# A key-limit step split from its product, an earlier transpose of v, and two turns less before the own exponentials

## The chip, the core and the metric

The kernel runs on one core of a Trainium2 chip. The metric is the device time of one execution in microseconds (us). The three executions before the change took 990.68, 991.01 and 991.49 us; their median, 991.01 us, is the time before.

## What is computed

Two independent results stand side by side in the output, 512 columns each.

```python
# A: attention with 32 query heads of 16 columns, one shared k and v (2048 rows)
q = (x @ wq) by heads;  k = x @ wk;  v = x @ wv
p = softmax(q @ k.T * 16 ** -0.5)
a = (p @ v, heads side by side) @ wo
# B: gated long convolution of 512 channels over 2048 rows
kv = short_conv(k, shift_k) * v          # 4 taps
b = q * (irfft(rfft(kv) * rfft(ssm_k)) + kv * ssm_D)
out = concatenate([a, b], -1)
```

## The kernel before

**Stacks, tiles and turns.** Attention is cut into 32 stacks (one for four heads and 512 queries). A stack has 16 key tiles of 128 keys, and each makes two score tiles of 128 x 1024. Line 1074 writes a score tile into one of two PSUM buffers "s" (eight matmuls), line 1092 takes its exponential on ScalarE (ACT), and line 1116 multiplies the result with v into a PSUM pair "f" (called `pv`). `attend` walks over the tiles: turn x emits the scores and the exponential of tile x + 2, then the `pv` work that a plan has put into this turn, and then calls `fill.turn`. So a turn is one exponential long, and 32 turns make a stack. Stacks 27 to 30 have only 30 tiles: there the exponentials of the last key tile are computed on VectorE (DVE) by the thread `own`, one stack ahead.

**Fill work.** Everything else (projections, the convolution, the output product) lives in eight generator threads. They yield what they want next: `(n, dve, NEW or CONT, grain)` asks for n units of TensorE work, `(0, dve)` asks for DVE work alone, and `(WAIT, t)` sleeps for 2t turns. `_Fill.turn` (line 1433) goes through the threads in a fixed order (`own` first, then `wo_heads`, `conv_pe`, `conv_short`, `rest_of_q`, `wo_part`, `conv_dve`, `spill`). TensorE work needs room in the turn; work marked NEW also needs that no other thread holds the pair and that a PSUM pair is taken to be free; DVE work needs a positive credit, which grows by 850 a turn and falls by what is charged.

**What sets the order on the chip.** The program order on each engine is the order in which the turns emit. TensorE and DVE take their instructions strictly in that order, so a matmul that needs a DVE result holds up all scores behind it. There are two "f" pairs: one collects the `pv` of the running stack, the other goes from one piece of fill work to the next.

**The places that the change touches.**

- `rest_of_q` in stack 0 (lines 902 to 959): k and v of all keys are finished. `k_chunk(c, bank, h)` (684) multiplies once on TensorE (687), and DVE cuts the result (693), rounds it (700) and writes the key tiles `kst` (702). `v_turn` (704) transposes v on TensorE (709, four transposes) and copies it on DVE (712). `read(less)` (679) sleeps until the planner's estimate of DVE, minus `less`, is due.
- The end of `rest_of_q` (lines 1008 to 1020): the guard of the last x block (306), then `k_max` (670): DVE multiplies and limits four columns (673), TensorE sums them over partitions (674), DVE takes the maximum (677) and finishes with 1018 and 1019. `flag` (1034) follows with three small DVE steps (1041 to 1043), and ten turns later a transpose (1047) and two more (1049, 1050). The prologue calls the same `k_max` at line 848.
- `own` (1155): for stack n in 27 to 30 it waits until slot 32 n - 32 + `OWN_AT` (1168), asks for keys on TensorE twice (1173), and computes on DVE (1174, 1175, 1185, 1188).
- Behind them: at the end of a stack DVE copies the `pv` pair out (1125, 1126), SyncE's queue (SP) stores it (1129); `heads` reads it back and scales it (1248 to 1260, with a load of r at 1255); `wo_part` multiplies with wo (273, by way of `halves`) and DVE scales the result (1312).

Of the kernel before, what the change touches and what calls it, by code (L numbers as in the profile page):

```python
# [14 lines left out]
ALU = mybir.AluOpType  # L15
# [4 lines left out]
P = 128  # L20
# [16 lines left out]
LIM = 10000.0  # L37
# [32 lines left out]
OWN = NKT - 1  # L70
CROWDED = (0, 64), (288, 352)
OWN_IN = (27, 28, 29, 30)
OWN_AT, OWN_PV = 14, 8


def _tables():
# [30 lines left out]
WAIT = -1.0  # L107
NEW, CONT = 0, 1


class _Emit:
# [555 lines left out]
                stop=n == 11 or (c, n) == (3, 7),  # L667
            )

    def k_max(self, b, km):  # L670

        kx = self.ks[:, 4:8]
        self.nc.vector.tensor_scalar(kx, self.msk[:, 291:295], km, LIM, ALU.mult, ALU.min)
        self.nc.tensor.matmul(b, self.msk[:, 0:P], kx, start=True, stop=True)

    def k_row(self, kmr, b):
        self.nc.vector.tensor_reduce(kmr, b, AX.X, ALU.max)
# [87 lines left out]
    def prologue(self):  # L765
# [67 lines left out]
        kh = self.wide()[:, 0, :]  # L833
# [7 lines left out]
        km, kmr = self.ks[:, 0:1], self.ks[:, 1:2]  # L841
# [3 lines left out]
        nc.scalar.activation(qa, cut, AF.Abs)  # L845
        st = self.w.tile([P, 2, 512], F16, tag="st", bufs=2, name=self.nm("st"))
        self.st[0] = st
        self.k_max(kh[:, 0:4], km)
        self.k_first(kb, 0, range(8, 12))
        self.k_row(kmr, kh[:, 0:4])  # L850
        wbn = self.wbn.rearrange("p a (e r) -> p a e r", e=2)[:, :, :, BR]
# [4 lines left out]
        for a in both:  # L856
            b = (self.wide if a else self.pair)()[:, 0, :]
# [44 lines left out]
    def rest_of_q(self):  # L902
# [17 lines left out]
        b = self.pair()  # L920
        sums, rows = b[:, 0, :], b[:, 1, :]
        self.k_chunk(1, rows, 0)
        yield from self.read(700)
        yield 3, 400, CONT, 3
        self.v_turn(slice(0, 96), sums)
        yield from self.read(0)
        yield 2, 1300, CONT, 2
        self.k_chunk(1, rows, 1)
        yield from self.read(700)
# [34 lines left out]
        km, kmr = self.ks[:, 2:3], self.ks[:, 3:4]  # L964
# [7 lines left out]
        while n < 12:  # L972
            g = yield 12 - n, 1400, CONT if n else NEW, 1
            if n == 0:
                b = self.bank()
# [6 lines left out]
        for c in range(4):  # L982
            if c > 1:
                yield from self.after(("x", c))
            for g in (0, 2):
# [5 lines left out]
                if c or g:  # L991
# [4 lines left out]
                    b = yield from self.halves(*work, 1, 1400)  # L996
# [14 lines left out]
            if c < 2:  # L1011
                self.xT[c + 2] = self.w.tile([P, 2, 4, 512], F16, tag="xt", bufs=2, name=f"xT{c + 2}")
        self.qn = 4, 0
        yield 1, 500, NEW, 1
        b = self.bank()[:, 0:4]
        self.k_max(b, km)
        self.k_row(kmr, b)
        v.scalar_tensor_tensor(kmr, self.ks[:, 1:2], -1.015, kmr, ALU.mult, ALU.add)
        v.tensor_scalar(self.gm[:, 3:4], kmr, 1000.0, None, ALU.mult)
# [608 lines left out]
```

## Time and profile before

| what | us |
|---|---|
| three executions, median | 991.01 |
| the profiled execution, its own time | 991.43 |
| its span, first to last instruction | 989.7 |
| ScalarE busy | 951.4 |
| TensorE busy | 941.1 |
| VectorE busy | 747.5 |
| GpSimd busy | 174.0 |

The span leaves out 1.7 us of the profiled execution's own time. A timeline row gives start, length, engine, line, operation, tiles written and read, how many instructions are merged into it, and in square brackets how long the engine had been idle before and whose result ended that. A row of the table by stretches gives the stretch, its length, the busy time of TensorE, its weight loads, VectorE, ScalarE and GpSimd with their instruction counts, then the granted TensorE clock, the share of the DMA engines and GB/s.

### The profile page before, as it was taken

Reading aid. Unit: us, or ns where it says so; the run is one execution under the profiler, and the core shown is the slowest. Engines: PE = TensorE matmul, PEld = TensorE weight load, DVE = VectorE, ACT = ScalarE, POOL = GpSimd, SP = SyncE. Lnnn points to the kernel's source line nnn. Section 1 sums busy time; section 2 is a strip of 40 time slices with the busy share of each in tenths; the row PEclk is TensorE's granted clock in tenths of the full one; section 3 lists DMA queues with packets and bytes.
Section 4 is the critical chain, followed back from the end, with each engine's and each line's share of the span. In section 5 each row is a group of like instructions: output and inputs, shape, how many; then the busy total and the mean of one; then the engine's idle time right before and its main releaser. Section 6 shows DMA issues by size and latency. Waiting matters only on the chain.

```text
span 989.7 us, 51425 instructions
## 1 busy us (share of the span) xinstructions
PE 941.1 (95%) x23565; PEld 463.0 (47%) x23565; DVE 747.5 (76%) x925; ACT 951.4 (96%) x1032; POOL 174.0 (18%) x321
## 2 busy tenths in 40 slices
PE   8999999989999999999899999999979999999996
PEld 5344454435544444444444455544434444444453
DVE  4448686989369989998896578799888936677753
ACT  5799999999999999999999999999979999999995
POOL 6041131411021000100543432000000122211000
PEclk9799999999999999999999999999989999999999
DMA  7153442332133212211543333011221232221101
GB/s 251 57 153 92 121 137 85 107 101 61 29 81 104 81 59 83 79 59 44 155 129 107 96 110 97 22 54 43 61 74 45 75 97 93 81 66 54 40 19 48
DMA packets 69205, 82.93 MB, mean 84 GB/s; under 512 B 20752, under 2 KB 58294, under 8 KB 68982
## 3 DMA queue, kind: packets, MB, share of 16 engines
q1 hardware_dynamic: 47558, 43.48, 14.0%
q0 software_dynamic: 20320, 35.46, 12.1%
q8 instruction: 186, 3.05, 1.3%
q10 hardware_dynamic: 1104, 0.64, 0.2%
q14 instruction: 37, 0.30, 0.1%
HBM read 54.46 MB, written 25.03 MB: 80 GB/s over the span
## 4 chain that ended last, share of the span: by engine, by line
PE 50%; ACT 36%; issue 7%; DVE 6%; DMA 1%; SPq 0%; ACTq 0%; DVEq 0%
ACT p L1092 35%; PE f L1116 23%; PE s L1074 15%; PE f L273 9%; DMA r<-rd 1%; DVE sp L188 1%; ACT xT L630 1%; DVE sp L456 0%; PE f L618 0%; PE f L662 0%; PE f L687 0%; DVE o L1260 0%; PE f L254 0%; DVE ao L1125 0%; ACT pfirst L1092 0%
## 5 line engine op out<-in xcount | busy, mean ns | idle before, releaser
L1092 ACT ACTIVATE p<-s 128x1024 f32<-128x1024 f32 x1008 | 929.9, 1069 | 13.9 <-PE s L1074 12.7
L1116 PE MATMUL f<-p,vx 64*32 64x512 f32 (+1 forms) x8832 | 545.1, 554 | 0.3 <-ACT p L1092 0.3
L1074 PE MATMUL s<-st,kst 49*32 49x512 f16 x8128 | 424.0, 382 | 32.5 <-ACT p L1092 26.8
L1074 PEld LDWEIGHTS <-kst 49*32 49x32 f16 x8192 | 199.0, 89 | 401.9 <-issue 352.9
L1116 PEld LDWEIGHTS f<-p,vx 64*32 64x32 f32 x8832 | 174.0, 106 | 24.7 <-issue 2.7
L313 DVE COPY sp<-f 128x1024 f32<-128x1024 f32 x32 | 39.1, 1222 | 62.1 <-PE f L273 62.1
L188 DVE TENSOR_TENSOR sp<-sp 128x2048 f32<-128x2048 f32 x36 | 82.3, 2287 | 0.9
L318 POOL DMA_DIRECT2D ff<-in_ff x64 | 35.2, 556 | 233.7 <-ACT p L1092 215.3
L273 PE MATMUL f<-wo,o 64*32 64x512 f16 x1440 | 56.2, 375 | 0.3 <-DVE wp L1312 0.2
L273 PE MATMUL f<-xT,wq 64*32 64x512 f16 x1344 | 51.0, 375 | 0.0
L1125 DVE COPY ao<-f 128x512 f32<-128x512 f32 (+1 forms) x33 | 22.2, 674 | 37.5 <-PE f L1116 37.2
L318 POOL DMA_DIRECT2D fi<-in_fi x32 | 17.4, 550 | 182.0 <-ACT p L1092 181.8
L188 DVE TENSOR_TENSOR sp<-sp,sp 128x2048 f32<-128x2048 f32 x19 | 43.4, 2286 | 0.4
L273 PE MATMUL f<-a,ff 64*32 64x256 f32 x1024 | 41.8, 377 | 0.0
L273 PE MATMUL f<-hT,ff 64*32 64x256 f32 x1024 | 40.8, 377 | 0.7 <-DVE hT L367 0.7
L491 POOL DMA_DIRECT2D out<-r x32 | 17.7, 558 | 127.3 <-DVE r L489 117.4
L273 PE MATMUL f<-sp,fi 64*32 64x256 f32 x1024 | 40.0, 376 | 0.0
L489 DVE TENSOR_TENSOR r<-f,q 128x512 f32<-128x512 f32 x16 | 11.0, 689 | 38.0 <-PE f L273 37.9
L428 DVE TENSOR_TENSOR a<-a,t 128x512 f32<-128x512 f32 x48 | 33.1, 690 | 1.5
L419 DVE TENSOR_TENSOR t<-kk,tpb 128x512 f32<-128x512 f32 (+1 forms) x50 | 33.0, 663 | 0.0
L346 POOL DMA_DIRECT2D hin<-in_B_ssm_k x32 | 21.0, 660 | 60.1 <-ACT p L1092 58.6
L1188 DVE SCALAR_TENSOR_TENSOR own<-own,own 128x1024 f32<-128x1024 f32 x24 | 29.4, 1224 | 0.7
(195 smaller groups left out, 790.4 us busy)
## 6 DMA issues: line engine op xcount, KB each, us to landing
ff<-in_ff POOLq DMA_DIRECT2D x64, 128.0 KB, 2.7
od<-ao SPq DMA_DIRECT2D x60, 128.0 KB
qd<-qp SPq DMA_DIRECT2D x48, 128.0 KB
st<-qd SPq DMA_DIRECT2D x62, 98.0 KB
kk<-in_B_k POOLq DMA_DIRECT2D x32, 128.0 KB, 2.6
v<-in_B_v POOLq DMA_DIRECT2D x32, 128.0 KB, 2.6
hin<-in_B_ssm_k POOLq DMA_DIRECT2D x32, 128.0 KB, 5.5
fi<-in_fi POOLq DMA_DIRECT2D x32, 128.0 KB, 2.9
```

The lines of the kernel that those rows point to most:

```text
L188: v.tensor_tensor(out, a, b, op)
L273: y = self.nc.tensor.matmul(out[j : j + 32, cols], w[r, j : j + 32], x[r], start=half == m == 0, stop=half == 1 and m == k - 1,)
L313: self.nc.vector.tensor_copy(out, self.both.rearrange("p i (q n) -> p i q n", q=2))
L318: self.paced(self.nc.gpsimd.dma_start(t[:, i], self.I[n][:, 2 * m2 + i]))
L346: self.paced(nc.gpsimd.dma_start(dst, src))
L419: nc.vector.tensor_tensor(out[:, n], kk[:, x], tap(i, n.stop - n.start), ALU.mult)
L428: nc.vector.tensor_tensor(a, a, t, ALU.add)
L1074: self.nc.tensor.matmul(s[j : j + 32, e, :], self.kst[k // 2][rows, k % 2 * P + j : k % 2 * P + j + 32], self.st[n][rows, a, cols], start= ...
L1092: self.exps[u % 4] = self.nc.scalar.activation(self.pt[u], s, AF.Exp, scale=LN2 * DH**-0.5 / SC / SC)
L1116: nc.tensor.matmul(self.acc[e][32 * j : 32 * j + 32, m], vx[rows, :], y, start=k == 0, stop=stop)
L1125: nc.vector.tensor_copy(a, self.acc[0][:, m])
L1188: v.scalar_tensor_tensor(g, g if i < 4 else y, c[i], y if i else x.bitcast(BF16), ALU.add, ALU.mult)
```

## The change

Three things are moved; no instruction is added or taken away.

- `k_max` is split: `k_lim` holds the DVE step, `k_max` only the product. At the end of `rest_of_q`, `k_lim` is emitted as DVE work alone, then the thread sleeps ten turns, and then the product is asked for. In the prologue the two follow each other as before.
- In stack 0, `v_turn` comes one turn after the first `k_chunk` of block 1, no longer when DVE's estimate is due; the `k_chunk` behind it waits for the estimate less 500, no longer for the whole.
- `OWN_AT` goes from 14 to 12.

```diff
-OWN_AT, OWN_PV = 14, 8
+OWN_AT, OWN_PV = 12, 8
...
-    def k_max(self, b, km):
-
-        kx = self.ks[:, 4:8]
-        self.nc.vector.tensor_scalar(kx, self.msk[:, 291:295], km, LIM, ALU.mult, ALU.min)
-        self.nc.tensor.matmul(b, self.msk[:, 0:P], kx, start=True, stop=True)
+    def k_lim(self, km):
+
+        self.nc.vector.tensor_scalar(self.ks[:, 4:8], self.msk[:, 291:295], km, LIM, ALU.mult, ALU.min)
+
+    def k_max(self, b):
+
+        self.nc.tensor.matmul(b, self.msk[:, 0:P], self.ks[:, 4:8], start=True, stop=True)
...
-        self.k_max(kh[:, 0:4], km)
+        self.k_lim(km)
+        self.k_max(kh[:, 0:4])
...
         self.k_chunk(1, rows, 0)
-        yield from self.read(700)
+        yield WAIT, 0.5, CONT
         yield 3, 400, CONT, 3
         self.v_turn(slice(0, 96), sums)
-        yield from self.read(0)
+        yield from self.read(500)
         yield 2, 1300, CONT, 2
         self.k_chunk(1, rows, 1)
...
         self.qn = 4, 0
-        yield 1, 500, NEW, 1
+        yield 0, 200
+        self.k_lim(km)
+        yield WAIT, 5
+        yield 1, 200, NEW, 1
         b = self.bank()[:, 0:4]
-        self.k_max(b, km)
+        self.k_max(b)
         self.k_row(kmr, b)
```

## The prediction, made before the changed kernel ran

> **What bounds the kernel now.** I read the page first, for the busy shares and the groups.
>
> ```profile
> PE 941.1 (95%) x23565; PEld 463.0 (47%) x23565; DVE 747.5 (76%) x925; ACT 951.4 (96%) x1032; POOL 174.0 (18%) x321
> ...
> L1092 ACT ACTIVATE p<-s 128x1024 f32<-128x1024 f32 x1008 | 929.9, 1069 | 13.9 <-PE s L1074 12.7
> ```
>
> ScalarE is busy for 96% of the span, with exponentials that nothing can shorten here. Only its idle time can be won: 13.9 us stand before the 1008 exponentials, nearly all of it waiting for scores. Where that idle time lies, the timeline of ScalarE alone says. It merges exponentials that follow each other without a gap.
>
> ```profile
> 33.64 2.02 ACT L1092 ACTIVATE p<-s 128x1024 f32<-128x1024 f32 x2 [0.53 <-PE s L1074]
> 36.36 1.02 ACT L1092 ACTIVATE p<-s 128x1024 f32<-128x1024 f32 x1 [0.70 <-PE s L1074]
> 38.50 1.02 ACT L1092 ACTIVATE p<-s 128x1024 f32<-128x1024 f32 x1 [1.11 <-PE s L1074]
> 41.17 1.94 ACT L1092 ACTIVATE p<-s 128x1024 f32<-128x1024 f32 x2 [1.65 <-PE s L1074]
> 43.73 1.02 ACT L1092 ACTIVATE p<-s 128x1024 f32<-128x1024 f32 x1 [0.62 <-PE s L1074]
> 45.56 8.59 ACT L1092 ACTIVATE p<-s 128x1024 f32<-128x1024 f32 x9 [0.81 <-PE s L1074]
> ```
> ```profile
> 740.34 1.02 ACT L1092 ACTIVATE p<-s 128x1024 f32<-128x1024 f32 x1 [4.29 <-PE s L1074]
> 742.47 1.94 ACT L1092 ACTIVATE p<-s 128x1024 f32<-128x1024 f32 x2 [1.11 <-PE s L1074]
> 744.68 217.13 ACT L1092 ACTIVATE p<-s 128x1024 f32<-128x1024 f32 x236 [0.27 <-PE s L1074]
> ```
>
> The reader is to see two places. In stack 0 the gaps add up to 0.53 + 0.70 + 1.11 + 1.65 + 0.62 + 0.81 = 5.42 us. At 740 us they add up to 4.29 + 1.11 + 0.27 = 5.67 us. Together that is 11.1 of the 13.9 us, and the change touches both. Behind 744.68, 236 exponentials run at 217.13 / 236 = 0.920 us each with no gap, so whatever is moved there is hidden.
>
> **Part A: the limit of the maximum.** The timeline of all engines around 740 us, then the stretches with the granted clock.
>
> ```profile
> 738.80 0.21 DVE L673 TENSOR_SCALAR ks<-msk,ks 128x4 f32<-128x4 f32 x1
> 739.06 0.59 PE L674 MATMUL f<-ks,msk 128*128 128x4 f32 x2 [4.23 <-DVE ks L673]
> 739.69 0.16 DVE L677 TENSOR_REDUCE ks<-f 128x1 f32<-128x4 f32 x1 [0.68 <-PE f L674]
> ```
> ```profile
> 733.79:737.21 3.42, 1.04 (x24) 0.20 (x8) 3.35 (x6) 2.25 (x3) 0.00 (x0) 1.00 0.23 60
> 737.21:740.62 3.41, 1.56 (x18) 0.89 (x26) 2.59 (x9) 0.28 (x1) 0.00 (x0) 0.50 0.26 79
> 740.62:744.03 3.41, 3.41 (x48) 0.99 (x40) 3.38 (x5) 2.30 (x3) 0.00 (x0) 0.50 0.00 0
> ```
>
> TensorE stood 4.23 us before the product, because its operand was queued on DVE behind the guard and all that DVE was late with. All scores stood behind it. With TensorE only 1.04 us busy in one stretch, the clock was halved for the next 6.8 us, which makes the 1.11 and 0.27 us gaps.
>
> After the change DVE takes L673 at the same place: the planner's credit (2200 charged for the guard in turn 757, 850 back per turn) lets the 200 through in turn 759, ahead of `conv_dve`. The thread wakes in turn 769 and the product follows there, some 6 us after L673 is done. The added wait is one of the planner, so no engine stands for it. The moved instructions are L673, two matmul records (0.59 us at half clock), L677, 1018, 1019, three DVE steps of `flag`, its transpose and two more steps; no DMA is among them, and no queue of SP or POOL is passed. The product lies in a turn without `pv`, beside the exponentials. If that cover were gone it would cost its 0.59 us. All 5.67 us go.
>
> What is late next? DVE does not get faster because TensorE no longer waits. These rows decide, from the timeline behind the stall.
>
> ```profile
> 749.89 0.69 DVE L1125 COPY ao<-f 128x512 f32<-128x512 f32 x1 [2.95 <-PE f L1116]
> ...
> 752.19 0.60 SPq L1255 DMA_DIRECT2D r<-rd  x1
> ...
> 756.00 0.69 DVE L1260 TENSOR_TENSOR o<-of,r 128x512 f16<-128x512 f32 x1 [0.93 <-DMA r<-rd]
> ```
> ```profile
> 774.49 1.28 DVE L1312 TENSOR_SCALAR wp<-f 128x512 f32<-128x512 f32 x2
> ```
> ```profile
> 775.82 0.63 PE L273 MATMUL f<-wo,o 64*32 64x512 f16 x16 [0.17 <-DVE wp L1312]
> ```
>
> DVE ran without a break from L673 to 749.89 - 2.95 = 746.94, but for the 0.68 us at L677. Freed of that wait and of six small steps that now come later (some 0.15 us each, as L677), it is done at about 746.94 - 1.55 = 745.4. The last `pv` of the stack comes 5.67 us sooner, at 744.2 (749.89 - 5.67), so the copies start 1.2 us late by ScalarE's time. The second load of r stands behind the store of these copies in SP's queue, 2.30 us after the copy's start, and lands 3.81 us later: 745.4 + 2.30 + 3.81 = 751.5, where 756.00 - 5.67 = 750.3 would be in step. From L1260 to L1312 DVE had no wait (774.49 - 756.00 = 18.49 us), so L1312 ends 1.2 us late too, and TensorE, which needs that pair (now for `flag`'s transpose in turn 796, with the next product of `wo_part` two turns later), waits 1.2 us where it waited 0.17. Of the extra 1.0 us the slack of two score buffers takes up some 0.3. I charge 0.7; bounds 0 and 1.2. **Part A: 5.67 - 0.7 = 4.9 us** won, between 1.2 (below) and 5.7.
>
> **Part B: v transposed one turn sooner.** The stretches around the stack 0 gaps, and the timeline there.
>
> ```profile
> 30.65:34.06 3.41, 2.08 (x38) 0.96 (x30) 1.93 (x5) 2.88 (x4) 0.00 (x0) 1.00 0.38 127
> 34.06:37.47 3.41, 3.41 (x34) 1.09 (x42) 1.68 (x4) 2.62 (x3) 0.00 (x0) 0.50 0.20 68
> 37.47:40.89 3.42, 3.42 (x34) 0.79 (x26) 0.31 (x1) 1.02 (x1) 0.00 (x0) 0.50 0.00 0
> 40.89:44.30 3.41, 3.41 (x56) 1.12 (x40) 2.15 (x4) 2.51 (x3) 0.00 (x0) 0.50 0.02 5
> ```
> ```profile
> 32.62 0.48 DVE L702 SCALAR_TENSOR_TENSOR kst<-kh,msk,kc 128x256 f16<-128x256 f16 x1
> 33.16 0.41 PE L1074 MATMUL s<-st,kst 49*32 49x512 f16 x8 [1.15 <-ACT pfirst L1092]
> 33.50 0.55 PE L709 MATMUL f<-ident,kv 96*128 96x96 f32 x4
> 33.98 0.61 PE L1074 MATMUL s<-st,kst 49*32 49x512 f16 x8
> 34.09 0.36 DVE L712 TENSOR_SCALAR vx<-f 128x192 f32<-128x192 f32 x1 [0.98 <-PE f L709]
> 34.52 1.22 PE L687 MATMUL f<-kv,msk 32*128 32x256 f32 x2
> 35.66 0.63 PE L1074 MATMUL s<-st,kst 49*32 49x512 f16 x8
> 36.06 1.94 PE L1116 MATMUL f<-pfirst,vx 64*32 64x512 f32 x16
> ```
> ```profile
> 44.40 0.69 PE L687 MATMUL f<-kv,msk 32*128 32x256 f32 x2
> ```
>
> In the stretch to 34.06 TensorE is busy for 2.08 of 3.41 us; then the clock is halved until 44.30, and TensorE, always busy from there, is the bound. The row of 33.16 names ScalarE, but the key tile that these scores need was ready only at 32.62 + 0.48 = 33.10: that is the wait, and it stays. The transposes do not need that tile. One turn sooner they fall into the 1.15 us gap, at about 32.3, and cost nothing; L712 follows L702 on DVE and is done at 33.5. `read(500)` then lets the `k_chunk` out in turn 6, and it runs at 33.5 to 34.2, at nearly full clock. The next scores run at 34.2 and 34.7 (before: 33.98 and 35.66), so the 0.70 us gap goes. The `pv` starts at 35.1 and ends, at half clock (1.7 us from start to the next start), at 36.8; the scores behind it come at 37.3 (before 38.5): a gap of 0.7 instead of 1.11.
>
> Now the clock. The stretch to 34.06 is as thin as before (the `k_chunk` for the scores of 33.98), so I take it that the clock still falls. The stretch from 34.06 to 37.47 then holds three times the scores and a whole `pv` without the slack of 34.05 to 36.06. Like the stretch from 40.89 to 44.30, behind which the clock rose, it is packed with such matmuls, not with the thin L687 (32 rows) of the two before it. I take it that the clock rises at 37.47. From there at full clock: two kv products and an L687 (1.0 us together, the L687 as in the row of 44.40), scores at 38.5 (a gap of 0.65), and then none to the exponential that starts at 45.56 now: it starts at 41.7. **Part B: 45.56 - 41.7 = 3.8 us.** Bounds: 1.5 if the clock stays halved for all three stretches, 4.8 if it never falls.
>
> The Trainium skill ("TensorE: Matmul & The Clock Gate", Part 1) says that the clock is set by free-running windows of about 3.4 us, and falls after an idle one. The lengths agree: 44.30 - 34.06 and 744.03 - 737.21 are three and two windows. "Idle" does not: the window before 34.06 was 61% busy, with no gap over 1.15 us. A page that took only idle windows into account would leave the fall in stack 0 unexplained, and part B at 1.5; the measured rows decide. Free-running also means that the edges can lie elsewhere in another execution, which would move part B anywhere within its bounds.
>
> **Part C: own exponentials.** The table of waits has this row.
>
> ```profile
> DVE own L1174 <- PE f L1074: 13.7, 7, 4.5
> ```
>
> DVE waits for these keys, seven times, and ScalarE has no gap anywhere behind 744.68. Two turns sooner moves 16 DVE steps and two key products a stack in time, all beside exponentials. I take 0, bounds -0.5 and +0.5: the slack is real, but one late PSUM pair could cost about half an exponential's 0.92.
>
> **Sum.** On the profiled execution: 991.43 - 4.9 - 3.8 = 982.7. It was 0.4 above the median of the runs shown, 991.01, so the forecast is 982.3.
>
> **Rivals.**
> 1. *The clock in stack 0 stays halved for all three windows.* For it: two of the three full windows did not lift it. Against: the new first window is packed. 991.0 - 4.9 - 1.5 = 984.6.
> 2. *It never falls in stack 0.* For it: 2.08 us busy is not far from a window that may count as busy. Against: the transposes lay in that same window before. 991.0 - 4.9 - 4.8 = 981.3.
> 3. *The stall at 740 is paid again.* If one more 2.2 us DVE step slips ahead of the copies of 749.89, the first `pv` of the next stack waits some 2 us for its pair and the clock falls again. Against: by the credit, that step comes out behind the copies. Part A is then 1.2 and the time 991.0 - 1.2 - 3.8 = 986.0.
> 4. *Slower: the own keys take the free pair ahead of the convolution's products.* If DVE is 4 us behind at those turns, the next product waits as at 739, at 5.7 us each. With two of the four stacks hit: 991.0 - 8.7 + 11.4 = 993.7; it decides from the second one on. Against: DVE waits for the keys, not the other way round.
> 5. *The change does not do what it says*: the moves fall into turns without room and land where they were. 990 to 991. Against: both turns have no `pv`.
>
> **How the numbers follow.** The forecast's case 0.49, rival 1 0.16, rival 2 0.12, rival 3 0.13, rival 5 0.06, rival 4 0.04. A measurement of this kernel can tell about 0.2%, 2 us, from no change. Faster holds the first four, 0.90; same 0.06; slower 0.04. The range goes from rival 2 with 0.5 less (part C) to rival 3 with 1 more: 980.8 to 987.0.
>
> **What would show it.** A: the row of L674 without a wait, ScalarE without a gap over 0.5 us near 740, no half clock near 737, and TensorE waiting for L1312 by about 1.2 us. B: L709 in the gap before the scores of 33.16, the gap of 0.70 gone, half clock from 34.06 to 37.47 only. C: L1174 some 2 us to 6 us sooner, and no gap on ScalarE behind it. I am wrong if DVE's lateness spreads behind 751, or if the clock windows fall otherwise.

## The result, and the profile after

The changed kernel takes 984.66 us (median of six executions, 982.94 to 986.29); the kernel before took 990.85 us beside it (six executions, 989.28 to 991.62). The ratio is 0.9938, with an interval of 0.9923 to 0.9952: 6.1 us won, between 4.8 and 7.6. The forecast was 982.3 us in a range of 980.8 to 987.0. The profiled execution took 985.13 us with a span of 983.4. Of the executions of the kernel before that were timed beside the experiments below, 60 are counted; three disturbed ones, of 1062 us and more, are left out.

The page of the changed kernel first, busy shares and the group of exponentials (line 1092 is now 1098, and the scores of 1074 are now 1080):

```profile
PE 937.5 (95%) x23564; PEld 462.2 (47%) x23565; DVE 747.8 (76%) x926; ACT 951.2 (97%) x1032; POOL 172.9 (18%) x321
```
```profile
L1098 ACT ACTIVATE p<-s 128x1024 f32<-128x1024 f32 x1008 | 929.6, 1069 | 8.1 <-PE s L1080 6.8
```

ScalarE's work is the same (951.2 us beside 951.4). Its idle time before the exponentials fell from 13.9 to 8.1 us, and that 5.8 us is nearly all of the 6.3 us between the two profiled executions (991.43 and 985.13). The timeline of ScalarE says which gaps went. Stack 0, and then the rows from 699 to 955 us:

```profile
33.43 1.02 ACT L1098 ACTIVATE p<-s 128x1024 f32<-128x1024 f32 x1 [0.75 <-PE s L1080]
35.13 1.94 ACT L1098 ACTIVATE p<-s 128x1024 f32<-128x1024 f32 x2 [0.68 <-PE s L1080]
37.70 1.02 ACT L1098 ACTIVATE p<-s 128x1024 f32<-128x1024 f32 x1 [0.62 <-PE s L1080]
40.36 1.94 ACT L1098 ACTIVATE p<-s 128x1024 f32<-128x1024 f32 x2 [1.64 <-PE s L1080]
42.92 1.03 ACT L1098 ACTIVATE p<-s 128x1024 f32<-128x1024 f32 x1 [0.62 <-PE s L1080]
44.51 8.59 ACT L1098 ACTIVATE p<-s 128x1024 f32<-128x1024 f32 x9 [0.56 <-PE s L1080]
```
```profile
699.32 70.76 ACT L1098 ACTIVATE p<-s 128x1024 f32<-128x1024 f32 x77
770.44 185.00 ACT L1098 ACTIVATE p<-s 128x1024 f32<-128x1024 f32 x201 [0.36 <-PE s L1080]
```

The 5.67 us at 740 are gone; 0.36 us at 770 are new. So part A brought 5.67 - 0.36 = 5.3 us in this execution. In stack 0 the gaps still add up to 0.75 + 0.68 + 0.62 + 1.64 + 0.62 + 0.56 = 4.87 us, where 5.42 stood before: part B brought 0.55 us here, not 3.8, and less than the forecast's lower bound of 1.5.

Why so little in stack 0 is read from the stretches with the granted clock. They are divided where the clock changed, and 3.41 us on from there:

```profile
29.34:32.75 3.41, 2.62 (x42) 1.06 (x39) 2.15 (x6) 3.05 (x4) 0.00 (x0) 1.00 0.37 125
32.75:36.16 3.41, 3.41 (x42) 1.22 (x43) 1.52 (x4) 2.05 (x3) 0.00 (x0) 0.50 0.29 98
36.16:39.57 3.41, 3.41 (x28) 0.79 (x12) 0.00 (x0) 1.94 (x3) 0.00 (x0) 0.50 0.00 0
39.57:42.99 3.42, 3.42 (x49) 1.29 (x56) 2.46 (x4) 2.01 (x3) 0.00 (x0) 0.50 0.02 5
42.99:46.40 3.41, 3.41 (x76) 1.31 (x60) 1.50 (x4) 2.85 (x4) 0.00 (x0) 1.00 0.00 0
```

The clock is again halved for three windows, but they begin at 32.75, not at 34.06. Of the shift, 0.42 us is a shorter prologue (the first exponential starts at 23.84, before at 24.26); the rest, 0.9 us, is another place of the window's edge against the work. The first halved window therefore begins before the `k_chunk` of the timeline below, which runs in 1.22 us where it takes 0.69 at full clock, and it ends in the middle of the first `pv`.

```profile
31.88 0.55 PE L711 MATMUL f<-ident,kv 96*128 96x96 f32 x4 [0.30 <-DVE kc L695]
32.73 0.63 PE L1080 MATMUL s<-st,kst 49*32 49x512 f16 x8 [0.30 <-ACT pfirst L1098]
33.29 1.22 PE L689 MATMUL f<-kv,msk 32*128 32x256 f32 x2
34.44 1.05 PE L1080 MATMUL s<-st,kst 49*32 49x512 f16 x16
35.26 1.93 PE L1122 MATMUL f<-pfirst,vx 64*32 64x512 f32 x16
```

The move itself did what it was meant to: the transposes (L711, before L709) stand in the gap ahead of the scores, and the `k_chunk` follows the scores at once.

Around 744 us the timeline shows the limit (L672), its product six microseconds later (L676), and the wait that is late next, at the transpose of `flag` (L1053):

```profile
737.74 0.22 DVE L672 TENSOR_SCALAR ks<-msk,ks 128x4 f32<-128x4 f32 x1
```
```profile
743.89 0.39 PE L676 MATMUL f<-ks,msk 128*128 128x4 f32 x2
```
```profile
769.70 0.27 PE L1053 MATMUL f<-ident,g 128*1 128x128 f32 x1 [0.82 <-DVE wp L1318]
```

The product waits for nothing. TensorE waits 0.82 us for L1318 (before: L1312) at the transpose, and 0.36 of it reaches ScalarE.

The wait is where the forecast put it, but it did not come by the forecast's way, a load of r that stands behind the store of the copies in SP's queue. Both loads of r (L1261, before L1255) are issued 3.4 us ahead of that store (L1135, before L1129), and VectorE does not wait for them, where it waited 0.93 us before:

```profile
742.09 1.24 SPq L1261 DMA_DIRECT2D r<-rd  x2
745.45 0.81 SPq L1135 DMA_DIRECT2D od<-ao  x2
```
```profile
748.53 0.69 DVE L1266 TENSOR_TENSOR o<-of,r 128x512 f16<-128x512 f32 x1
```

VectorE's rows from 733 to 770 us show no idle time at all, so what TensorE waits for at the transpose is VectorE's own backlog.

For part C the table of waits has this row:

```profile
DVE own L1180 <- PE f L1080: 13.2, 8, 4.1
```

VectorE waits 13.2 us for the own keys, before 13.7, and there is no gap on ScalarE beside them. Counted in exponentials that have started, the first key products of the four stacks come behind 850, 880, 910 and 946 of them, before behind 852, 886, 916 and 946: two, six, six and no turns sooner.

### The profile page after: what moved, and what is told of

The parts are those of the page before. It is cut to its first block, busy times and chain, and to the rows that moved or that the text cites. A ratio compares the mean times of both kernels' runs of the same rounds, so it can differ in the third digit from the quotient of the medians.

```text
span 983.4 us, 51425 instructions
## 1 busy us (share of the span) xinstructions
PE 937.5 (95%) x23564; PEld 462.2 (47%) x23565; DVE 747.8 (76%) x926; ACT 951.2 (97%) x1032; POOL 172.9 (18%) x321
## 3 DMA queue, kind: packets, MB, share of 16 engines
q8 instruction: 186, 3.05, 1.3%
## 4 chain that ended last, share of the span: by engine, by line
PE 50%; ACT 39%; issue 7%; DVE 4%; ACTq 0%; DVEq 0%
ACT p L1098 38%; PE f L1122 22%; PE s L1080 15%; PE f L273 10%; DVE sp L188 0%; PE f L618 0%; PE f L662 0%; PE f L689 0%; PE f L254 0%; ACT xT L630 0%; ACT pfirst L1098 0%; PE f L625 0%; PE x L625 0%; DVE u L241 0%; DVE o L1266 0%
## 5 line engine op out<-in xcount | busy, mean ns | idle before, releaser
L188 DVE TENSOR_TENSOR sp<-sp 128x2048 f32<-128x2048 f32 x35 | 80.0, 2287 | 0.9
L192 DVE TENSOR_TENSOR sp<-sp 128x1024 f32<-128x1024 f32 x26 | 30.8, 1215 | 0.0
```

What stands on the lines that cost most here:

```text
L188: v.tensor_tensor(out, a, b, op)
L192: v.tensor_tensor(part(out), part(a), part(b), op)
```

## The experiments

Two questions were left: what each part is worth by itself, and whether part B is small, or only was small where the clock's windows happened to lie. Theory: part A brings its 5 us whenever it runs, while part B is worth something between 0.6 and 4.8 us that each execution draws anew. Rival: part B is worth its 0.6 us, and all of the rest is part A.

**The limit and the own keys, without the move of v.**

```diff
         self.k_chunk(1, rows, 0)
-        yield WAIT, 0.5, CONT
+        yield from self.read(700)
...
-        yield from self.read(500)
+        yield from self.read(0)
```

> The change without the earlier transposes of v. Theory: the stall of 4.23 us at the limit and the two gaps behind it at half clock (5.67 us on ScalarE) are nearly all that the change wins; TensorE then waits 0.8 us for line 1312 at 770 and ScalarE 0.36 us. So 990.85 - 5.3 = 985.5 us, with no gap over 0.5 us near 740. Rival (the prediction's sizes): 4.9 us, 986.0, and the transposes carry another 3.8.

984.94 us (981.53 to 985.97), ratio 0.9936, interval 0.9912 to 0.9959. On the 990.74 us of before beside it this is 6.3 us, between 4.1 and 8.7. ScalarE has no gap from 217 us to 800 us:

```profile
215.32 1.02 ACT L1098 ACTIVATE p<-s 128x1024 f32<-128x1024 f32 x1 [1.36 <-PE s L1080]
217.45 583.33 ACT L1098 ACTIVATE p<-s 128x1024 f32<-128x1024 f32 x634 [1.10 <-PE s L1080]
```

The expected 0.36 us at 770 is not there: TensorE waits 0.37 us for L1318, and none of it reaches ScalarE. Part A, together with the own keys, stands by itself, and its 6.3 us are no less than the 6.1 (4.8 to 7.6) of the whole change in its first set. The same rows hold a surprise: 1.36 + 1.10 us of gaps near 216, where the changed kernel has one of 0.74. Nothing in this kernel differs there from the one before; the clock fell for one window at 213.81 in this execution.

**The move of v alone.** The rest is as before; the own turns are 14.

> The earlier transposes of v alone. Theory: the clock still falls in stack 0 for three windows, so the gap of 0.70 us goes and little else: 0.6 to 1.0 us, about 990.0 us. Rival (the prediction): the clock rises again after one window, 3.8 us, 987.0 us. Where the window edges lie differs from one execution to the next, so single times should spread by 2 to 3 us.

988.28 us (986.36 to 991.86, twelve executions), ratio 0.9975, interval 0.9960 to 0.9991: 2.5 us, between 0.9 and 4.0; the theory gave 0.6 to 1.0. The stall at 740 is there, as it must be:

```profile
737.28 1.02 ACT L1096 ACTIVATE p<-s 128x1024 f32<-128x1024 f32 x1 [3.82 <-PE s L1078]
739.41 1.94 ACT L1096 ACTIVATE p<-s 128x1024 f32<-128x1024 f32 x2 [1.11 <-PE s L1078]
741.92 32.19 ACT L1096 ACTIVATE p<-s 128x1024 f32<-128x1024 f32 x35 [0.56 <-PE s L1078]
```

So on the mean part B is worth more than the 0.55 us of the first profile. The forecast's 3.8 still lies inside the interval. In this profile the clock was halved for two windows, where the theory expected three. The stall, 3.82 + 1.11 + 0.56 us here and 5.67 before, is not the same in every execution either: in the profile of the next kernel, which has it too, the three gaps are 2.91 + 0.43 + 0.62 = 3.96 us, with one halved window.

**The own keys alone.** `OWN_AT` is 12, everything else as before.

> Own exponentials two turns sooner, alone. Both theories: no change, 990.9 us within 0.5, DVE line 1174 some 2 us or more sooner and no gap on ScalarE behind 745 us. Rival: a pair taken too early costs a gap of 0.5 us or more behind 810 us.

990.49 us (985.92 to 992.79, twelve executions), ratio 0.9996, interval 0.9978 to 1.0014. But the expected shift of line 1174 (here 1178) did not come: its first row starts at 825.52, before at 825.64, and the key products stand behind the same 852, 886, 916 and 946 exponentials. VectorE, ScalarE, GpSimd and SyncE carry out the same instructions in the same order as before. Without the other two moves the new `OWN_AT` moves nothing, so this run is a second measurement of the kernel before and not a test of part C. What the earlier keys do by themselves is not shown.

**The whole change again,** as a second set.

> The whole change again, on the chip of the next two runs, as their yardstick: 984.7 us, single times 982 to 987. Theory: single times follow the time at half clock (span times twice what the granted clock lacks), about 0.3 to 0.4 us for each us of it; rival: they do not.

982.05 us (980.01 to 987.04), ratio 0.9919, interval 0.9894 to 0.9943. The profiled execution of this set is the one that the forecast described. Its stretches, and stack 0 on ScalarE:

```profile
30.97:34.38 3.41, 2.62 (x39) 1.20 (x32) 2.11 (x6) 2.88 (x4) 0.00 (x0) 1.00 0.40 135
34.38:37.79 3.41, 3.41 (x42) 0.85 (x42) 1.33 (x3) 2.47 (x4) 0.00 (x0) 0.50 0.18 59
37.79:41.20 3.41, 3.34 (x61) 1.12 (x59) 2.17 (x4) 2.88 (x4) 0.00 (x0) 1.00 0.00 0
```
```profile
24.50 3.23 ACT L1098 ACTIVATE pfirst<-s 128x1024 f32<-128x1024 f32 x3 [0.57 <-PE s L1080]
```
```profile
42.35 8.59 ACT L1098 ACTIVATE p<-s 128x1024 f32<-128x1024 f32 x9 [0.16 <-PE s L1080]
```

One halved window, and 42.35 - 24.50 = 17.85 us from the first exponential to the row of nine. Before it was 45.56 - 24.26 = 21.30: 3.45 us won, beside a forecast of 3.8. In the first profile of the same program it was 44.51 - 23.84 = 20.67, 0.6 us won. The program is the same; the edge lay at 34.38 here and at 32.75 there.

The kernel without the move draws its edge as well, so two such lengths are only to be compared where the edges lie alike. Each trace has a record of the granted clock, and it gives the edge at which the clock fell. The table counts that edge from the first exponential, and gives the number of halved windows in stack 0 and the length up to the row of nine:

| edge, us | v at its old place | v moved |
|---|---|---|
| 8.8 to 8.9 | 2 windows, 19.77 (limit and own keys) | 3 windows, 20.67 (changed kernel), 20.75 (thin matmuls, below) |
| 9.5 to 10.0 | 3 windows, 21.30 (before), 21.32 (own keys alone) | 1 window, 17.85 (changed kernel, second set), 17.77 (two turns, below) |
| 11.1 | no profile | 2 windows, 19.48 (move of v alone), 19.48 (six more at the start, below) |

With the edge at 9.5 to 10.0 the move wins 3.5 us. With the edge at 8.9 it loses 0.9. Only one or two profiles stand in each field. So the move decides how many windows are halved, but which way depends on the edge, and the 0.6 us of the first profile compared two different edges. Part B has no single size; its mean, 2.5 us (0.9 to 4.0) with the move alone, speaks narrowly against the rival's 0.6.

The theory stated for this set holds. Over the twelve executions of the changed kernel the time follows the time at half clock with a correlation of 0.91 and 0.44 us for each us; over the 60 executions of before beside the experiments it is 0.88 and 0.40. Before spends 18.8 us at half clock on the mean and the changed kernel 9.2. So of the 7.1 us between their means about 9.6 x 0.40 = 3.8 go with the half clock.

**Full matmuls into the pair in use.** If thin work lets the clock fall, full work in the same place should hold it. Three and four products of 128 x 128 with 256 columns were put behind the transposes and behind the `k_chunk`, into parts of the same PSUM pair that are overwritten or not used.

```diff
         self.v_turn(slice(0, 96), sums)
+        self.stuff(rows[:, 256:512], 3, 128, 128)
         yield from self.read(500)
         yield 2, 1300, CONT, 2
         self.k_chunk(1, rows, 1)
+        yield WAIT, 0.5, CONT
+        self.stuff(rows[:, 0:256], 4, 128, 128)
```

> The whole change, and in stack 0 seven matmuls of 128 x 128 by 256 columns whose result nobody reads: three behind the transposes of v, four one turn behind the next key chunk (0.11 us each at full clock). Theory: the clock falls because too little of the array works in one window, so this extra work keeps it up: full clock through 33 to 43 us, the gaps of ScalarE in stack 0 shrink from 4.9 to about 1.5 us, time 981.3 us. Rival: what counts is the order of waits, or the longest gap; the clock falls all the same and the extra work costs up to 0.8 us: 984.7 to 985.5 us.

987.71 us (984.89 to 990.24, twelve executions), ratio 0.9974, interval 0.9960 to 0.9989: more than the 984.66 and 982.05 of the change without them. The experiment was badly laid out, as its timeline shows:

```profile
33.05 0.49 PE L624 MATMUL f<-xT 128*128 128x256 f16 x3 [0.57 <-DVE vx L720]
```
```profile
35.21 1.01 PE L624 MATMUL f<-xT 128*128 128x256 f16 x4 [0.37 <-DVE kc L701]
```

Both groups waited for VectorE, which was still reading the other half of the pair, and they stand ahead of the scores. So a new wait was added, and the question of the clock not answered.

**Full and thin matmuls into a free pair.** Now six products, three ahead of the transposes and three behind, into a pair that nobody reads: once with the full array (128 rows, 128 columns), once with 32 x 32 of it.

```diff
+        d = self.pf.tile([P, 2, 512], F32, tag="f", name=self.nm("d"))
+        self.stuff(d[:, 0, 0:256], 3, 128, 128)
         self.v_turn(slice(0, 96), sums)
+        self.stuff(d[:, 0, 0:256], 3, 128, 128)
```

> The whole change, and in stack 0 six matmuls of 128 x 128 by 256 columns that nobody reads, into the free PSUM pair, so that none of them waits for DVE: three ahead of the transposes of v and three behind, in the two gaps of 0.30 us. Theory: a window is judged by how much of the array works; this adds 0.64 us of the whole array to the thin window and the clock falls in fewer executions: 982.5 us, at half clock 4 to 6 us less than the whole change. Rival: only idle time counts, and then these six matmuls help as much as thin ones do (next run).

> As the run before, but each extra matmul has 32 rows and 32 columns, a sixteenth of the array, for the same 0.11 us. Theory: nothing is won over the whole change, 984.7 us, the clock falls as before. Rival (busy time counts): the same 982.5 us as the run before.

The full ones: 985.2 us (983.32 to 986.51), ratio 0.9940, interval 0.9924 to 0.9955. The thin ones: 987.38 us (982.65 to 990.87, twelve executions), ratio 0.9954, interval 0.9936 to 0.9973. In the profiled execution with the full ones the clock never fell in stack 0; in the one with the thin ones it fell from 32.66 to 42.90, three windows. Over all executions the time at half clock is 2 to 8 us with the full ones, 4.9 on the mean; that is 4.3 us less than the 9.2 of the change alone, and 4 to 6 were expected; with the thin ones it is 2 to 20, 9.9 on the mean. So the clock holds in some executions with thin ones too. Both times are longer than expected (982.5 and 984.7). Stack 0 in the trace with the full ones:

```profile
33.52 3.82 ACT L1107 ACTIVATE p<-s 128x1024 f32<-128x1024 f32 x4 [0.53 <-PE s L1089]
37.65 2.85 ACT L1107 ACTIVATE p<-s 128x1024 f32<-128x1024 f32 x3 [0.31 <-PE s L1089]
40.67 8.59 ACT L1107 ACTIVATE p<-s 128x1024 f32<-128x1024 f32 x9 [0.16 <-PE s L1089]
...
301.90 256.73 ACT L1107 ACTIVATE p<-s 128x1024 f32<-128x1024 f32 x279 [0.86 <-PE s L1089]
560.41 208.19 ACT L1107 ACTIVATE p<-s 128x1024 f32<-128x1024 f32 x226 [1.78 <-PE s L1089]
```

The row of nine starts at 40.67, with 24.15 for the first exponential: 16.52 us, 4.78 less than before. The upper bound of part B was 4.8. Yet the time did not fall below that of the change alone, since two gaps are new, at 302 and 560 us, far from the edit (two smaller ones, of 0.51 and 0.59 us, stand at 769 and 782). The kernel with thin products has them too (1.09 and 1.51 us), and the kernel with the fill in the used pair has the second (2.06 us near 560). No kernel without added products has one over 0.25 us there.

**Where those gaps come from.** The later program is the same, but each later instruction of TensorE has another number. Three kernels tell that apart. The first has no fill; two of its ten warm-up products of the first 5 us are cut into quarters, which adds six products and no array work.

```diff
-        self.warm(self.pair()[:, 1, :], zero, 10)
+        wp = self.pair()
+        self.warm(wp[:, 1, :], zero, 8)
+        self.warm(wp[:, 1, 0:P], zero[:, 0:P], 8)
```

> The changed kernel with two of its ten warm-up products of the first 5 us cut into four quarters each: the same array work, but six more products (and weight loads) in TensorE's program, ahead of everything. Nothing else differs. Theory 1 (the gaps of the filled kernels near 302, 560 and 782 us come from where the later instructions lie in TensorE's stream, since six more instructions moved them): the same gaps show here, above all 1 to 2 us near 560 with TensorE waiting for the load of ff, and the time is some 3 us over the changed kernel's, 985.5 to 988. Theory 2 (they come from something else in those kernels, the extra PSUM pair or chance): no gap over 0.5 us on ScalarE between 290 and 730 us, and 982 to 985. Both: stack 0 lasts 17.5 to 21 us, by the edges of the clock's windows.

The other two have the fill as three wide products (512 columns) into a free pair; in the last, three warm-up products are taken away in exchange, so that behind stack 0 the count is that of the changed kernel.

```diff
-        self.warm(self.pair()[:, 1, :], zero, 10)
+        self.warm(self.pair()[:, 1, :], zero, 7)
...
+        d = self.pf.tile([P, 2, 512], F32, tag="f", name=self.nm("d"))
+        self.warm(d[:, 0, :], self.xT[0][:, 0, 0, :], 2)
         self.v_turn(slice(0, 96), sums)
+        self.warm(d[:, 0, :], self.xT[0][:, 0, 0, :], 1)
```

> The changed kernel with three full products of 128 x 512 around the transposes of v in turn 5 of stack 0, into a free pair: the same array work as the six products of 256 columns, with three more instructions in TensorE's stream instead of six. All theories: the clock does not fall in stack 0, which lasts 16.5 us. Theory 1 (position in the stream): the gaps near 302, 560 and 782 may move or go with another count, so the time may be anything from 980 to 985. Theory 2: as the six products, 985, with the gap near 560.

> As the kernel with three full products around the transposes, but with three warm-up products fewer at the start, so that behind stack 0 each instruction of TensorE has the same number as in the changed kernel. Theory 1 (position in the stream): no gap near 302, 560 or 782, stack 0 lasts 16.5 us, the half clock there is gone, and the time is 3 us under the changed kernel's mean of 983.4: 980 to 981.5. Theory 2 (what the added products bring is lost again whatever the count): a gap of 1 to 2 us near 560 and 984 to 986. A prologue that runs at a lower clock for want of three warm-up products would cost up to 1 us in both.

Six more at the start: 986.73 us (982.63 to 990.29, twelve executions), ratio 0.9963, interval 0.9946 to 0.9980. The time is in the range of theory 1, and the gaps near 302 and 560 are there; the one near 782 is not. ScalarE, and then TensorE at the second of them:

```profile
304.62 256.71 ACT L1100 ACTIVATE p<-s 128x1024 f32<-128x1024 f32 x279 [0.82 <-PE s L1082]
562.83 208.02 ACT L1100 ACTIVATE p<-s 128x1024 f32<-128x1024 f32 x226 [1.50 <-PE s L1082]
```
```profile
561.87 0.42 PE L273 MATMUL f<-a,ff 64*32 64x256 f32 x4 [1.20 <-DMA ff<-in_ff]
```

TensorE waits for the load of `ff`. Wide, three more: 983.52 us (982.78 to 985.18), ratio 0.9935, interval 0.9914 to 0.9955, no such gaps, but two of 1.02 and 1.11 us at 212 to 214 and three of 0.26 to 0.73 us at 744 to 748, both groups at a halved clock. In stack 0 the clock held. Wide, same count: 982.32 us (980.20 to 985.20), ratio 0.9928, interval 0.9905 to 0.9950. ScalarE behind stack 0 of the last one:

```profile
49.71 161.29 ACT L1101 ACTIVATE p<-s 128x1024 f32<-128x1024 f32 x173 [0.29 <-PE s L1083]
211.74 738.82 ACT L1101 ACTIVATE p<-s 128x1024 f32<-128x1024 f32 x803 [0.74 <-PE s L1083]
950.73 15.21 ACT L1101 ACTIVATE p<-s 128x1024 f32<-128x1024 f32 x16 [0.17 <-PE s L1083]
```

Three gaps in 900 us, and the clock held in stack 0. So the gaps at 302 and 560 go with the position of the later instructions in TensorE's stream, and not with the fill. The expected 980 to 981.5 us was not reached by the median, though by three of the six executions. With the clock held in stack 0 and no such gaps, this kernel still is not measurably faster than the change alone, whose two sets have medians of 984.66 and 982.05.

The traces say more about the one at 560. The pages of the profile list a DMA queue called `instruction`, with 186 packets and 3.05 MB, 16 KiB each. In the four kernels with that gap one such packet starts 2.3 to 2.9 us after the first of the four `ff` loads there is issued; in the nine others none starts before 3.4 us. A load lands in sixteen parts. In the kernel with six more at the start, fifteen parts of the second load are there 3.03 us after that issue and the last one at 4.60, and TensorE starts right behind it. In the nine kernels without the gap the first two loads are complete by 3.3 us. So the position decides whether a packet of instructions meets a load that TensorE is about to need. This fits all thirteen traces, but that the packet is what holds up the late part is inferred. At 302 it is something else: in the three kernels with that gap TensorE's weight loads stop for 0.88 to 1.15 us within a `pv`, and the profile names nothing that they wait for. That cause stays open.

**Two turns in place of ten.**

```diff
         self.k_lim(km)
-        yield WAIT, 5
+        yield WAIT, 1
         yield 1, 200, NEW, 1
```

> The whole change, but the product follows its limit after two turns and not ten. Theory: DVE takes the limit at its old place, so TensorE reaches the product about 3 us sooner than DVE is done with it less two turns of 0.92 us: a wait of 1.5 to 2.5 us at about 737, ScalarE idle for 1.2 to 2.3 us there. Rival (the wait came from the pair or the product itself, not from DVE's queue): no wait, or the old 4.2 us.

One execution: 983.3 us. The expected wait of 1.5 to 2.5 us is not there, which is the outcome that the rival named. But the rival's reason is not what the trace shows: the weights of L676 wait 0.38 us for L672, so VectorE's queue still comes last, only by less, and ScalarE has no gap near 735. The price comes later. The timeline 17 us behind:

```profile
748.72 2.29 DVE L188 TENSOR_TENSOR sp<-sp,sp 128x2048 f32<-128x2048 f32 x1
...
750.93 0.27 DVE L1055 TENSOR_REDUCE g2m<-f 1x1 f32<-1x128 f32 x1
...
751.26 0.63 PE L273 MATMUL f<-wo,o 64*32 64x512 f16 x16 [1.60 <-DVE g2m L1055]
...
752.23 3.94 ACT L1098 ACTIVATE p<-s 128x1024 f32<-128x1024 f32 x4 [1.36 <-PE s L1080]
```

The whole tail of the step comes sooner. The maximum behind the transpose of `flag` (L1055) now queues behind a 2.29 us step of VectorE and holds the pair that the next product needs: 1.36 us on ScalarE, where ten turns pay 0.36 in the first profile and nothing in the second. In this execution two of the ten turns were enough to free the product; the others keep `flag` away from VectorE's busy turns. It is one execution, so only the row is evidence, not the time.

## Why the prediction was right, point by point

- **Part A was right in its cause and nearly in its size.** 4.9 us was forecast, 5.3 measured in the first profile, and 6.3 (4.1 to 8.7) without the move of v, where the own keys are moved too. The product without a wait, no halved clock near 737 and the wait for the scaling step at `flag`'s transpose came where they were named.
- **The way to that wait was wrong.** The forecast had the copies 1.2 us late, the second load of r behind their store, and so L1260 and L1312 1.2 us late. The copies do start one turn late: 0.69 us into the 771st exponential, before 0.67 us into the 770th. But the loads of r are ahead of the store, and L1266 comes 0.7 us earlier against the exponentials than L1260 did. L1318 is then 0.6 us late, behind VectorE's other work. TensorE waited 0.82 us, and 0.57 in the second profile; 0.36 and nothing reached ScalarE, where 0.7 was charged.
- **Rival 3 and rival 4 did not happen, and rival 5 did for a part.** The stall was not paid again, and no product waited for the own keys. With the own keys alone the move landed where it was; in the whole change three of four stacks have their keys two to six turns sooner, without a gap on ScalarE. Part C by itself was not measured, so its forecast of 0 is not tested.
- **Part B's steps on the engines were right, its size was not.** The forecast took the edge of the window as fixed at 34.06, and so a first halved window filled with scores and a whole `pv`. That is the step that failed: "I take it that the clock rises at 37.47". With the edge at 32.75 the first halved window held the thin `k_chunk` as well, and did not lift the clock, so rival 1's condition held in the profiled execution, and less was won than the 1.5 us that it allowed. With the edge at 34.38, as far behind the first exponential as the forecast's own, the forecast's case came out, 3.45 us for 3.8. With the clock held by full products the upper bound came out, 4.78 for 4.8.
- **The forecast knew this and did not act on it.** It said that free-running windows could put part B anywhere within its bounds, and then took the edges of one trace for its likeliest time. It also left out that the kernel before draws its edge too, so that the move can lose: 0.9 us with the edge at 8.9. The two sets of the changed kernel stand at 984.66 and 982.05; that the second lies so near to 982.3 is in part a matter of edges.
- **What stays open.** The parts measured alone, 6.3 and 2.5 us, are 8.8 together, where the whole change won 6.1 and 8.0 in its two sets; intervals of 1.4 to 2.4 us to each side cover this. The full clock in stack 0 shortened it by 4.78 us in the trace, and the kernel that holds it with the count unchanged is not measurably below the change alone. The 60 executions of before beside the experiments lie between 986.03 and 995.0 us. Only the profiled ones show where their windows lie.

## What to carry to other kernels

Split a small step from the matmul that reads it, and give it turns of its own: the queue of the in-order engine, not the step's 0.2 us, is what it costs. Ask also what the moved tail will meet, as the two-turn version shows. See in the trace that an edit tried alone moves what it is meant to move. A gain that hangs on where the clock's windows fall has to be priced over all places of the edge, its single profile is to be read as one draw, and two profiles are to be compared only with their edges alike; when the count of instructions changes too, take a control with the same count before a distant gap is put down to the edit.

## What was not expected of the hardware

- **A halved clock comes in pieces of 3.41 us, with edges that differ between executions of one program** (32.75 and 34.38 for the changed kernel, 8.9 and 9.9 us behind the first exponential). The Trainium skill ("TensorE: Matmul & The Clock Gate", Part 1) says that the windows are free-running, and the traces agree. It also says that the clock falls after an idle window, and there they do not: the window before the fall was busy for 2.62 of 3.41 us in both profiles of the changed kernel.
- **Busy time does not say when the clock falls.** In the profile of before, whose edge of 34.06 comes again after 52 windows at 211.56, this stretch keeps the clock, and so does the next:

```profile
211.56:214.97 3.41, 1.92 (x47) 0.52 (x24) 2.29 (x6) 3.41 (x5) 1.06 (x2) 1.00 0.12 34
214.97:218.38 3.41, 3.39 (x88) 1.79 (x89) 3.38 (x8) 2.62 (x3) 0.00 (x0) 1.00 0.58 165
```

  1.92 us busy was enough there, 2.62 us were not in stack 0. (With another edge the clock fell near there too, at 213.81 without the move of v.) What fills the time differs (scores and `pv` there; beside scores the transposes, products of 32 rows and other small shapes here), and six products of the full array held the clock where six of 32 x 32 did not. The full products held it in all three profiles that have them in a free pair, with an edge at 9.4, 10.3 and 11.4 us behind the first exponential, counted back from later edges in steps of 3.413 us; without them it fell in stack 0 in all nine, at 8.8 to 11.1, one of them at 9.5. That the share of the array at work counts fits all of this, but it is not shown: the edges could not be set, and some executions without full products have hardly any half clock (2 us in one with the thin ones, and in one with the limit and the own keys alone).
- **Six more products in the first 5 us cost time 300 and 560 us later.** The gaps of 0.82 and 1.50 us came with the count of instructions ahead and went when the count was restored. The Trainium skill ("Runtime: NRT & Kernel Launch", section "Instruction fetch mechanics") says that the program is streamed in blocks of 16 KiB and that the cost of crossing one is mostly hidden. The packets of 16 KiB in the queue `instruction` agree with the first; at 560 us the second did not hold, if the load came late for the reason inferred above.
